# A conv-then-gated-MLP kernel: a reworked opening (tap broadcast, first cast, band copies, order of the first loads, first transposes)

## The chip, the cores and the metric

The kernel runs on one core of a Trainium2 chip. The metric is the device time of one execution in microseconds (us). Below, PE is the matrix engine, PEld its weight loads, DVE the vector engine, ACT the scalar engine, POOL is GpSimd, and SP the engine that only issues transfers here. "L415" is line 415 of the kernel before.

## What is computed

```
w   = softmax(weight, over the 7 taps)                  # weight [8 heads, 7]
y[b, s, c] = sum_k w[c // 24, k] * x[b, s - 6 + k, c]   # causal, zeros ahead of s = 0
h   = y.reshape(32768, 192) @ w_in                      # w_in [192, 2048]
out = (h * cos(h)) @ w_out                              # w_out [2048, 192], float32 result
```

x is [8, 4096, 192] float32. The reference adds 1e-9 to the softmax sum. The kernel computes in bf16 with float32 accumulation.

## The kernel before

The 32768 rows are cut into 64 tiles of T = 512 rows, and two tiles make a unit of 1024 rows; a unit has eight blocks of 128 rows. For each tile PE does eight first products h0 to h7 (`mm1`, L488; each takes 6 matmuls of 512 columns and fills two PSUM banks with 256 of the 2048 hidden features), ACT takes the cosine of each as Sin(h + pi/2) (L510), DVE multiplies (L514), and PE adds the second product in 64 steps (`mm2_step`, L523; steps 0 to 15 need the first half of w_out, step 16 is the first that needs the second half). What PE does in which order is written out by hand in strings (PE_FIRST for the first tiles, PE_ORDER later): "h3" is a first product, "m11" eleven steps of the second, "d11" or "c11" a part of the convolution of unit 1, "r" the second half of that of unit 0, "w5" five filler matmuls, "K1" two casts of unit 1 on POOL, "W0" and "W1" the casts of the halves of w_out on POOL, "X0" a DMA transpose of the second half of unit 0. ACT_FIRST and ACT_ORDER do the same for ACT ("s3" is the cosine of h3, "er" and "ed11" copies of the convolution out of PSUM).

The convolution is a product with a banded 128 x 256 matrix for each head (`band`), whose entries are the softmaxed taps. Units 0 to 3 are done on PE; the later ones are split between PE and POOL and are not touched by the change.

The change concerns what comes ahead of the first h0, called the opening here. In order:

- L80-81: ACT's queue loads the 56 taps as 4 rows of 14 (`w_row`); SP's queue loads the first four blocks of unit 0 (L102, called x0a here).
- L128-136: DVE clears `zero`; `keep_warm(n)` is n filler matmuls of 512 columns on it.
- L139-151: POOL makes `quarter` [4, 128] (a memset and two selects), PE runs three fillers, then one float32 matmul spreads the four rows of taps over the four quarters of 32 partitions (`w_all`), then nine fillers.
- L156-164: POOL makes `mask` on 32 partitions, DVE and ACT copy it to the other three quarters (ACT twice).
- L111-112, L165: POOL issues the two loads of w_in, which cast to bf16 on the way. L167-171: POOL clears a block and makes `ident`.
- L175-185: DVE and ACT do the softmax (max, subtract, Exp, sum, reciprocal, multiply into `wn`); ACT loads the Sin table behind its Exp.
- L398: ACT casts x0a to bf16. L400-404: DVE multiplies mask by taps (`prod`) and adds up (`diag`).
- L406-410: SP waits for `diag`, then issues the rest of unit 0 (called x0b here), unit 1 in two halves and its edges.
- L412-416: 16 copies of 32 x 76 put `diag` into `band`, four for each pair of heads (the pairs are taken one after another): the letters of "DPDPDPDPDPDPDPAA" give the engine (D for DVE, P for POOL, A for ACT).
- L417-421: POOL casts x0b and makes `pick`.
- `conv_first` (L426): PE convolves the first four blocks, in two halves of 16 matmuls; the first half needs all four pairs of heads of `band`. ACT copies half 0 out and DVE half 1 (L438), each value twice, into the two sets of columns t of `ct_tiles[0]`. SP waits for DVE's copy and then issues the four loads of w_out (L442-443, L124).
- `turn_first` (L445): PE transposes each block with three matmuls against `ident` (L453; the doubled values make all 128 output rows), ACT and DVE copy the result into cT (L457). Then the tiles begin: "K1 h0a h0b W0 h1 ...", where h0a and h0b are the two halves of h0.

All transfers issued by SP go through one queue in the order of issue.

Of the kernel before, what the change touches and what calls it, by code (L numbers as in the profile page):

```python
# [8 lines left out]
FP32 = mybir.dt.float32  # L9
# [7 lines left out]
def kernel(  # L17
# [61 lines left out]
    HQ = H // 4  # L79
    w_row = consts.tile([4, HQ * K], FP32)  # L80
    nc.scalar.dma_start(out=w_row, in_=weight.rearrange("(q h) k -> q (h k)", q=4))

# [44 lines left out]

    one = consts.tile([128, 1], FP32)  # L128
    nc.vector.memset(one, 1.0)
# [4 lines left out]
    def keep_warm(n, bank=idle):  # L134
        for _ in range(n):
            nc.tensor.matmul(out=bank, lhsT=zero[:, 0:128], rhs=zero, start=True, stop=True)  # L136


    quarter = consts.tile([4, 128], FP32)  # L139
    nc.gpsimd.memset(quarter, 1.0)  # L140
    nc.gpsimd.affine_select(out=quarter, in_=quarter, compare_op=ALU.is_ge, fill=0.0, base=0, pattern=[[1, 128]],
                            channel_multiplier=-32)
    nc.gpsimd.affine_select(out=quarter, in_=quarter, compare_op=ALU.is_ge, fill=0.0, base=31, pattern=[[-1, 128]],
                            channel_multiplier=32)
    scrap = consts.tile([128, 1], FP32)
    nc.scalar.activation(out=scrap, in_=one, func=AF.Exp)
    keep_warm(3)
    w_all = o_pools[1].tile([128, T], FP32, name="o_ps1")
    w_bc = w_all[:, 0 : HQ * K].rearrange("p (h k) -> p h k", k=K)
    nc.tensor.matmul(out=w_all[:, 0 : HQ * K], lhsT=quarter, rhs=w_row, start=True, stop=True)  # L150
    keep_warm(9)

# [26 lines left out]
    nc.scalar.activation(out=wexp, in_=wexp, func=AF.Exp)  # L179
    nc.scalar.activation(out=scrap, in_=one, func=AF.Sin)  # L180
    wsum = consts.tile([128, HQ, 1], FP32)
# [170 lines left out]
    def taps(u, j, half, mul):  # L352
        if u not in pa:
            pa[u] = pa_pool.tile([128, PA, WN, OR], FP32, name="pa")
        part = slice(HALF * half, HALF * (half + 1))
        mul(pa[u][:, j, part], tap_window(u, j)[:, part], tap[:, j : j + 1])  # L356
# [3 lines left out]
    def conv_raw(u):  # L360

        a, p = pa.pop(u), raw_prod
# [34 lines left out]

    cast_unit(0, 0, NB, nc.scalar.copy)  # L398

# [3 lines left out]
    diag = consts.tile([128, HQ, E], FP32)  # L403
    summed = nc.vector.tensor_reduce(out=diag, in_=prod, axis=mybir.AxisListType.X, op=ALU.add)  # L404

    tc.add_manual_dep(nc.sync.nop().ins, summed.ins.name, sync_dep, reason="order of the transfers")  # L406
    load_unit(0, NB, UB)
    load_unit(1, 0, NB)
    load_unit(1, NB, UB)
    load_edges(1)  # L410

    three = {"D": nc.vector.tensor_copy, "A": nc.scalar.copy, "P": nc.gpsimd.tensor_copy}  # L412
    for i, k in enumerate("DPDPDPDPDPDPDPAA"):
        q, rows = divmod(i, 4)
        three[k](out=band[32 * rows : 32 * rows + 32, HQ * q : HQ * (q + 1), 32 * rows : 32 * rows + E],  # L415
                     in_=diag[32 * q : 32 * q + 32])
    cast_unit(0, NB, UB)  # L417
# [8 lines left out]
    def conv_first():  # L426

        banks = o_banks()
        for half in range(2):
            for h in range(H):  # L430
                for prev in range(2):
                    nc.tensor.matmul(  # L432
                        out=banks[half][:, 0 : 2 * D].rearrange("p (n k h r) -> p h n k r", n=2, k=NC, h=H)[:, h],
                        lhsT=band[:, h, 128 * prev : 128 * prev + 128],
                        rhs=bf[0][:, 2 * half + 1 - prev : 2 * half + 3 - prev, h * G : (h + 1) * G].rearrange(
                            "p n (k r) -> p n k r", k=NC),
                        start=(h == 0 and prev == 0), stop=(h == H - 1 and prev == 1), skip_group_check=True)
            m = copies[half](out=ct_tiles[0][:, 2 * half : 2 * half + 2].rearrange("p n k t w -> p (n k) t w"),  # L438
                             in_=banks[half][:, 0 : 2 * D].rearrange("p (m t w) -> p m t w", t=1, w=64).to_broadcast(
                                 [128, 2 * NC, 2, 64]))  # L440
        tc.add_manual_dep(nc.sync.nop().ins, m.ins.name, sync_dep, reason="order of the transfers")
        load_wo(0)  # L442
        load_wo(1)

    def turn_first(half):  # L445
        for n in range(2):
            last = half and n
            ps = [o_pools[0].tile([128, T], FP32, name="o_ps0")] if last else ring_banks()
            if n == 0:
                keep_warm(2 - half, ps[1])  # L450
            ps = ps[0]
            for k in range(NC):
                nc.tensor.matmul(out=ps[:, k * 128 : (k + 1) * 128],  # L453
                                 lhsT=ct_tiles[0][:, 2 * half + n, k, :, :].rearrange("p t w -> p (t w)"), rhs=ident,
                                 start=True, stop=True, skip_group_check=True)
            m = NC * (2 * half + n)
# [131 lines left out]

    PE_ORDER = ['m12 h0 m4 h1 K+3 R+1 m5 h2 m7 q h3 U+0 m6 h4 m17 h5 X+1 m9 p h6 h7 O m4', 'm11 h0 m4 h1 m6 h2 m7 q x+1 h3 m5 h4 m7 c1 m8 c2 m3 h5 T+3 L+4 m9 p O h6 h7 m4']
    ACT_ORDER = ['s0 s1 a211 s2 s3 s4 a014 a114 Q s5 P s6 s7 a007', 's0 s1 s2 a102 s3 a203 s4 Q ec2 ec1 s5 P s6 s7']  # L590

    PE_FIRST = ["K1 h0a h0b W0 h1 h2 h3 r h4 w5 d11 w4 h5 d21 W1 c11 X0 m1 h6 m11 h7 L2 c21 D1",
# [5 lines left out]
    ACT_FIRST = ["s0a s0b s1 s2 er s3 s4 ed11 ed21 s5 ec11 s6 ec21 s7",  # L598
                "s0 s1 s2 s3 s4 s5 ec12 ec22 Q P s6 ed12 s7 ed22 ec13 ec23",
                "s0 s1 s2 s3 Q s4 P s5 s6 s7",  # L600
                "s0 s1 s2 s3 s4 ed13 ed23 Q s5 P s6 s7"] + ACT_ORDER

    PE_LAST = "m10 h0 m3 h1 m13 h2 m2 q h3 m10 h4 m3 h5 m7 h6 m12 p h7 O m7"
    ACT_LAST = "s0 s1 s2 s3 s4 s5 s6 P A s7"
# [7 lines left out]
    for t in range(NT + 1):  # L612
        u, second = divmod(t, TPU)
        cu = u + TPU
        if t >= 2 * TPU:
            if second:
                conv["c"] = conv_unit(cu, ring_banks) if cu < NU else iter(())
        pe = PE_LAST if t == NT - 1 else "m%d p" % (2 * STEPS * NT - step) if t == NT else PE_ORDER[second] if t >= len(PE_FIRST) else PE_FIRST[t]
        act = ACT_LAST if t == NT - 1 else ACT_ORDER[second] if t >= len(ACT_FIRST) else ACT_FIRST[t]
# [6 lines left out]
        def flush():  # L626
            while act:
                k = act[0]
                if k[0] == "e":
                    need = k[1:] if k[1:] in conv else k[1] + "2" + k[3:]  # L630
                else:
                    need = "p" if k in "PQA" else "h" + k[3:] if k[0] in "ab" else "h" + (k[1:2] if k[2:] in "lr" else k[1:])
                if need not in done:
# [5 lines left out]
                elif k[0] in "ab":  # L639
                    if u + 2 in rT:  # L640
                        taps(u + 2, int(k[1]), int(k[2]), nc.scalar.mul if k[0] == "a" else nc.vector.tensor_scalar_mul)
                elif k[0] == "e":
# [20 lines left out]
        for k in pe.split():  # L663
# [5 lines left out]
            elif k[0] == "m":  # L669
                for q in range(step, step + int(k[1:])):  # L670
                    mm2_step(q)
                step += int(k[1:])
            elif k[0] == "w":
                keep_warm(int(k[1:]), o_pools[0].tile([128, T], FP32, name="o_ps0"))
            elif k == "p":
                assert step % (2 * STEPS) == 0
                made = step // (2 * STEPS) - 1
            elif k == "q":
                assert step % (2 * STEPS) == STEPS
            elif k[0] == "W":  # L680
# [11 lines left out]
            flush()  # L692
            if k == "p" and made == NT - 1:
                finish(NT - 1)
        assert t == NT or not act
# [30 lines left out]
```

## Time and profile before

| | us |
|---|---|
| median of 3 runs | 705.16 (705.04 to 705.51) |
| the profiled execution, its own time | 705.18 |
| its span, first to last instruction | 703.5 |
| PE busy | 697.0 (99%) |
| ACT busy | 644.4 (92%) |
| DVE busy | 642.4 (91%) |
| POOL busy | 503.7 (72%) |
| first matmul of h0 | 10.60 after the start of the span |
| step 16 of the second product | 22.64 after the start of the span |

The span is divided by the profile into lines of instructions with a start, a duration, an engine, a line of the kernel and, in brackets, how long the engine was idle ahead of it and what ended that. The chain of waits is followed back from the last instruction: at each step to what released it, or to the instruction before it on its engine. The granted clock of PE was 0.999 of full speed over the span.

### The profile page before, as it was taken

To read this page: it belongs to the slowest core of one execution; us is meant where nothing else is said; L and a number is where in the kernel's file an instruction comes from. 1 tells how busy PE (TensorE), PEld (TensorE's weight loads), DVE (VectorE), ACT (ScalarE), POOL (GpSimd) and SP (SyncE) were. 2 spreads that over 40 slices of the span, in tenths; PEclk is the share of its full clock that TensorE was granted. 3 is DMA by queue.
4 is the path that set the end of the run, shared out by engine and by line. 5 is a ranking of instruction groups with operands and counts; after the bars stand their busy time and mean duration, and the time that the engine had idled before them with its cause. 6 is when DMAs were issued, how large, how long until landed. Compare 5 with 4: busy or idle time off the path is not lost.

```text
span 703.5 us, 26826 instructions
## 1 busy us (share of the span) xinstructions
PE 697.0 (99%) x11830; PEld 512.8 (73%) x11830; DVE 642.4 (91%) x598; ACT 644.4 (92%) x831; POOL 503.7 (72%) x214
## 2 busy tenths in 40 slices
PE   8999999999999999999999999999999999999997
PEld 4677777777777777777777777777777777777776
DVE  6889999999999999999999999999999999999996
ACT  7889999999999999999999999999999999999875
POOL 6524478977778877778877688877789778799400
PEclk9999999999999999999999999999999999999999
DMA  8964456667667768676656577577665576874331
GB/s 214 234 167 97 120 135 143 138 147 164 138 153 146 131 145 176 134 152 131 147 152 153 150 159 129 140 161 150 143 147 132 145 174 137 153 127 95 92 91 47
DMA packets 228292, 100.09 MB, mean 142 GB/s; under 512 B 156240, under 2 KB 227792, under 8 KB 228176
## 3 DMA queue, kind: packets, MB, share of 16 engines
q1 hardware_dynamic: 227464, 97.40, 62.7%
q8 instruction: 92, 1.51, 0.9%
q0 software_dynamic: 416, 0.79, 0.7%
q14 instruction: 24, 0.20, 0.1%
q10 hardware_dynamic: 296, 0.20, 0.1%
HBM read 31.36 MB, written 25.17 MB: 80 GB/s over the span
## 4 chain that ended last, share of the span: by engine, by line
PE 96%; DMA 1%; DVE 1%; POOL 0%; SPq 0%; ACT 0%; issue 0%; POOLq 0%
PE o_ps L552 48%; PE h L503 46%; PE h L277 2%; DMA wo_f<-in_moe_w_out_dram 1%; PE h L552 0%; SPq L124 0%; PE h L229 0%; DVE band L415 0%; POOL wo L120 0%; POOL mask L159 0%; DVE ct L438 0%; PE o_ps L432 0%; ACT mask L164 0%; DVE diag L404 0%; DVE prod L401 0%
## 5 line engine op out<-in xcount | busy, mean ns | idle before, releaser
L514 DVE TENSOR_TENSOR g<-h,cs 128x1024 bf16<-128x1024 f32 (+1 forms) x513 | 604.9, 1216 | 27.9 <-ACT cs L510 24.5
L510 ACT ACTIVATE cs<-h 128x1024 bf16<-128x1024 f32 (+1 forms) x513 | 511.0, 1021 | 44.0 <-PE h L503 30.6
L552 PEld LDWEIGHTS <-g 64*128 64x128 bf16 x8192 | 354.2, 94 | 102.2 <-issue 1.0
L552 PE MATMUL o_ps<-wo,g 64*128 64x192 bf16 x8128 | 420.6, 243 | 0.1
L503 PE MATMUL h<-cT,w 64*128 64x512 bf16 (+1 forms) x3078 | 407.0, 376 | 0.8 <-DVE g L514 0.4
L503 PEld LDWEIGHTS <-w 64*128 64x128 bf16 x3078 | 147.6, 94 | 75.0 <-issue 1.8
L211 POOL CAST xk<-x_f 128x768 bf16<-128x768 f32 (+1 forms) x56 | 76.4, 1367 | 113.9 <-DMA x_f<-in_x_dram 109.3
L363 POOL TENSOR_TENSOR raw_prod<-rT,tap 128x2784 f32<-128x2784 bf16 x28 | 135.3, 4832 | 0.2
L370 POOL TENSOR_TENSOR raw_prod<-raw_prod,pa 128x2088 f32<-128x2088 f32 x28 | 129.1, 4609 | 2.2
L356 ACT ACTIVATE pa<-rT,tap 128x348 f32<-128x348 bf16 x168 | 94.6, 580 | 0.0
L374 POOL TENSOR_TENSOR raw_prod<-raw_prod 128x1392 f32<-128x1392 f32 x28 | 87.9, 3138 | 2.2
L571 DVE COPY o_sb<-o_ps 128x384 f32<-128x384 f32 x62 | 34.6, 557 | 23.7 <-PE o_ps L552 23.5
L377 POOL TENSOR_TENSOR ro<-raw_prod 128x696 bf16<-128x696 f32 x28 | 46.5, 1660 | 2.2
L294 ACT CAST ct_buf<-h 112x480 bf16<-112x480 f32 x56 | 28.6, 562 | 4.1 <-PE h L277 0.6
L571 ACT COPY o_sb<-o_ps 128x384 f32<-128x384 f32 x64 | 30.8, 482 | 0.1
L277 PE MATMUL h<-xk,band 64*112 64x120 bf16 x448 | 21.2, 213 | 0.0
L277 PEld LDWEIGHTS <-band 64*112 64x112 bf16 x448 | 18.0, 127 | 0.0
L219 POOL CAST x_bf<-x_f 128x768 bf16<-128x768 f32 (+2 forms) x5 | 9.1, 1812 | 7.0 <-DMA x_f<-in_x_dram 6.9
L307 POOL COPY ct<-ct 128x1728 bf16<-128x1728 bf16 x3 | 4.9, 1630 | 8.9 <-ACT ct L239 8.9
L394 POOL COPY cT<-cT 128x144 bf16<-128x144 bf16 x3 | 0.9, 308 | 13.5 <-DMA cT<-ct 13.5
L136 PE MATMUL o_ps<-zero 128*128 128x512 bf16 x21 | 7.2, 492 | 1.3 <-DVE zero L131 1.3
L239 ACT CAST ct<-h 128x432 bf16<-128x432 f32 x12 | 5.9, 530 | 0.4 <-issue 0.4
(66 smaller groups left out, 52.7 us busy)
## 6 DMA issues: line engine op xcount, KB each, us to landing
out_dram<-o_sb SPq DMA_DIRECT2D x63, 384.0 KB, 3.7
x_f<-in_x_dram SPq DMA_DIRECT2D x28, 480.0 KB, 5.5
x_f<-in_x_dram SPq DMA_DIRECT2D x56, 192.0 KB, 2.7
cT<-ro SPq DMA_DIRECT2D x112, 87.0 KB, 2.3
x_f<-in_x_dram SPq DMA_DIRECT2D x4, 384.0 KB, 5.6
wo_f<-in_moe_w_out_dram SPq DMA_DIRECT2D x4, 384.0 KB, 7.9
x_f<-in_x_dram SPq DMA_DIRECT2D x2, 768.0 KB, 5.2
cT<-ct_buf SPq DMA_TRANSPOSE x56, 4.0
```

Source lines behind the costliest of these rows:

```text
L211: copy(out=xk[u][:, NC * n0 : NC * n1].rearrange("p (k n) m -> p k n m", k=NC), in_=x_tiles[u][:, n0:n1].rearrange("p n (m k) -> p k n m", ...
L277: return nc.tensor.matmul(out=ps[h // 4][0:OP, 0 : NPB * 4 * G].rearrange("p (m i r) -> p i m r", m=NC * NPB, i=4)[:, h % 4], lhsT=band[si ...
L356: mul(pa[u][:, j, part], tap_window(u, j)[:, part], tap[:, j : j + 1])
L363: nc.gpsimd.tensor_tensor(out=p, in0=tap_window(u, PA, K), in1=tap[:, PA:K].rearrange("p (j a b) -> p j a b", a=1, b=1).to_broadcast([128, ...
L370: add(out=p[:, 0:m], in0=p[:, 0:m], in1=a[:, done : done + m], op=ALU.add)
L374: add(out=p[:, 0:m], in0=p[:, 0:m], in1=p[:, n - m : n], op=ALU.add)
L377: add(out=ro[u], in0=p[:, 0], in1=p[:, 1], op=ALU.add)
L503: nc.tensor.matmul(out=h[:, i, n0 * 128 : n1 * 128], lhsT=w[rows, k, j, :], rhs=rhs, start=(k == 0), stop=(k == NC - 1))
L510: nc.scalar.activation(out=cs[:, :, part], in_=h[:, :, part], func=AF.Sin, bias=math.pi / 2.0, scale=1.0)
L514: nc.vector.tensor_tensor(out=g_tiles[t][:, 2 * j : 2 * j + 2, part], in0=h[:, :, part], in1=cs[:, :, part], op=ALU.mult)
L552: ms.append(nc.tensor.matmul(out=o_ps[tt, b, si], lhsT=g_tiles[tt][rows, f, s * 128 : (s + 1) * 128], rhs=wo[rows, f // 2, f % 2, :], star ...
L571: (copy or copies[b])(o_sb[t][:, 2 * b : 2 * b + 2, :].rearrange("p s d -> p (s d)"), o_ps.pop((t, b)))
```

## The change

- The taps are loaded into one partition as a row of 4 x 14. `quarter` and its three POOL instructions go; four float32 matmuls, one for each quarter of 32 output partitions, with a row of 32 ones as weights, take the place of the one. Eleven fillers follow, where there were nine.
- x0a is cast by POOL, where it was ACT.
- The 16 band copies go to DVE, ACT and POOL as "DAPDAPDAPDAPDADA" (6, 6 and 4), where it was 7, 2 and 7.
- SP's loads of x0b and unit 1 wait for the last band copy, where they waited for `diag`.
- `conv_first` copies each value out once (384 elements for each partition, where it was 768).
- `turn_first` transposes each block of 64 columns twice, into the output rows 0-63 and 64-127, so 24 matmuls with 64 columns of weights where there were 12 with 128. One filler stands ahead of each half, where there were two and one.
- The marks "p" and "q" in the order strings go; the end of a second product is found by counting steps. The order in which instructions are issued from the first tile on stays as it was.

```
-    w_row = consts.tile([4, HQ * K], FP32)
-    nc.scalar.dma_start(out=w_row, in_=weight.rearrange("(q h) k -> q (h k)", q=4))
+    w_row = consts.tile([1, 4, HQ * K], FP32)
+    nc.scalar.dma_start(out=w_row, in_=weight.rearrange("(o q h) k -> o q (h k)", o=1, q=4))
...
-    one = consts.tile([128, 1], FP32)
+    one = consts.tile([128, 32], FP32)
...
-    quarter = consts.tile([4, 128], FP32)
-    nc.gpsimd.memset(quarter, 1.0)
-    nc.gpsimd.affine_select(out=quarter, ...)
-    nc.gpsimd.affine_select(out=quarter, ...)
...
-    nc.tensor.matmul(out=w_all[:, 0 : HQ * K], lhsT=quarter, rhs=w_row, start=True, stop=True)
-    keep_warm(9)
+    for q in range(4):
+        nc.tensor.matmul(out=w_all[32 * q : 32 * q + 32, 0 : HQ * K], lhsT=one[0:1], rhs=w_row[:, q], start=True, stop=True)
+    keep_warm(11)
...
-    cast_unit(0, 0, NB, nc.scalar.copy)
+    cast_unit(0, 0, NB)
...
-    summed = nc.vector.tensor_reduce(out=diag, in_=prod, axis=mybir.AxisListType.X, op=ALU.add)
-    tc.add_manual_dep(nc.sync.nop().ins, summed.ins.name, sync_dep, reason="order of the transfers")
+    nc.vector.tensor_reduce(out=diag, in_=prod, axis=mybir.AxisListType.X, op=ALU.add)
+    three = {"D": nc.vector.tensor_copy, "A": nc.scalar.copy, "P": nc.gpsimd.tensor_copy}
+    for i, k in enumerate("DAPDAPDAPDAPDADA"):
+        q, rows = divmod(i, 4)
+        m = three[k](out=band[32 * rows : 32 * rows + 32, HQ * q : HQ * (q + 1), 32 * rows : 32 * rows + E],
+                     in_=diag[32 * q : 32 * q + 32])
+    tc.add_manual_dep(nc.sync.nop().ins, m.ins.name, sync_dep, reason="order of the transfers")
     load_unit(0, NB, UB)
     load_unit(1, 0, NB)
     load_unit(1, NB, UB)
     load_edges(1)
-    three = {...}
-    for i, k in enumerate("DPDPDPDPDPDPDPAA"):
...
-            m = copies[half](out=ct_tiles[0][:, 2 * half : 2 * half + 2].rearrange("p n k t w -> p (n k) t w"),
-                             in_=banks[half][:, 0 : 2 * D].rearrange("p (m t w) -> p m t w", t=1, w=64).to_broadcast(
-                                 [128, 2 * NC, 2, 64]))
+            m = copies[half](out=ct_tiles[0][:, 2 * half : 2 * half + 2, :, 0].rearrange("p n k w -> p (n k) w"),
+                             in_=banks[half][:, 0 : 2 * D].rearrange("p (m w) -> p m w", w=64))
...
-                keep_warm(2 - half, ps[1])
+                keep_warm(1, ps[1])
...
-                nc.tensor.matmul(out=ps[:, k * 128 : (k + 1) * 128],
-                                 lhsT=ct_tiles[0][:, 2 * half + n, k, :, :].rearrange("p t w -> p (t w)"), rhs=ident,
-                                 start=True, stop=True, skip_group_check=True)
+                for i in range(2):
+                    nc.tensor.matmul(out=ps[64 * i : 64 * i + 64, k * 128 : (k + 1) * 128],
+                                     lhsT=ct_tiles[0][:, 2 * half + n, k, 0, :], rhs=ident,
+                                     start=True, stop=True, skip_group_check=True)
```

More of the change, by code (lines that the diff above doesn't have):

```diff
@@ L136, in keep_warm @@
             nc.tensor.matmul(out=bank, lhsT=zero[:, 0:128], rhs=zero, start=True, stop=True)
-    quarter = consts.tile([4, 128], FP32)
-    nc.gpsimd.memset(quarter, 1.0)
[L141 to L144, printed above, removed]
     scrap = consts.tile([128, 1], FP32)
-    nc.scalar.activation(out=scrap, in_=one, func=AF.Exp)
+    nc.scalar.activation(out=scrap, in_=one[:, 0:1], func=AF.Exp)
     keep_warm(3)
@@ L179 @@
     nc.scalar.activation(out=wexp, in_=wexp, func=AF.Exp)
-    nc.scalar.activation(out=scrap, in_=one, func=AF.Sin)
+    nc.scalar.activation(out=scrap, in_=one[:, 0:1], func=AF.Sin)
     wsum = consts.tile([128, HQ, 1], FP32)
@@ L354, in taps @@
             pa[u] = pa_pool.tile([128, PA, WN, OR], FP32, name="pa")
+        have.add(("tap", u, j, half))
         part = slice(HALF * half, HALF * (half + 1))
@@ L360, in conv_raw @@
     def conv_raw(u):
+        assert {("tap", u, j, half) for j in range(PA) for half in range(2)} <= have
         a, p = pa.pop(u), raw_prod
@@ L410 @@
     load_edges(1)
-    three = {"D": nc.vector.tensor_copy, "A": nc.scalar.copy, "P": nc.gpsimd.tensor_copy}
-    for i, k in enumerate("DPDPDPDPDPDPDPAA"):
-        q, rows = divmod(i, 4)
-        three[k](out=band[32 * rows : 32 * rows + 32, HQ * q : HQ * (q + 1), 32 * rows : 32 * rows + E],
-                     in_=diag[32 * q : 32 * q + 32])
     cast_unit(0, NB, UB)
@@ L584 @@
     o_ps, o_sb, turns, evacs = {}, {}, {}, set()
-    PE_ORDER = ['m12 h0 m4 h1 K+3 R+1 m5 h2 m7 q h3 U+0 m6 h4 m17 h5 X+1 m9 p h6 h7 O m4', 'm11 h0 m4 h1 m6 h2 m7 q x+1 h3 m5 h4 m7 c1 m8 c2 m3 h5 T+3 L+4 m9 p O h6 h7 m4']
+    PE_ORDER = ['m12 h0 m4 h1 K+3 R+1 m5 h2 m7 h3 U+0 m6 h4 m17 h5 X+1 m9 h6 h7 O m4', 'm11 h0 m4 h1 m6 h2 m7 x+1 h3 m5 h4 m7 c1 m8 c2 m3 h5 T+3 L+4 m9 O h6 h7 m4']
     ACT_ORDER = ['s0 s1 a211 s2 s3 s4 a014 a114 Q s5 P s6 s7 a007', 's0 s1 s2 a102 s3 a203 s4 Q ec2 ec1 s5 P s6 s7']
     PE_FIRST = ["K1 h0a h0b W0 h1 h2 h3 r h4 w5 d11 w4 h5 d21 W1 c11 X0 m1 h6 m11 h7 L2 c21 D1",
[5 rows of a table removed]
[5 rows of a table added]
     ACT_FIRST = ["s0a s0b s1 s2 er s3 s4 ed11 ed21 s5 ec11 s6 ec21 s7",
@@ L600 @@
                 "s0 s1 s2 s3 Q s4 P s5 s6 s7",
-                "s0 s1 s2 s3 s4 ed13 ed23 Q s5 P s6 s7"] + ACT_ORDER
-    PE_LAST = "m10 h0 m3 h1 m13 h2 m2 q h3 m10 h4 m3 h5 m7 h6 m12 p h7 O m7"
[3 rows of a table added]
+    PE_LAST = "m10 h0 m3 h1 m13 h2 m2 h3 m10 h4 m3 h5 m7 h6 m12 h7 O m7"
     ACT_LAST = "s0 s1 s2 s3 s4 s5 s6 P A s7"
@@ L617 @@
                 conv["c"] = conv_unit(cu, ring_banks) if cu < NU else iter(())
-        pe = PE_LAST if t == NT - 1 else "m%d p" % (2 * STEPS * NT - step) if t == NT else PE_ORDER[second] if t >= len(PE_FIRST) else PE_FIRST[t]
+        pe = PE_LAST if t == NT - 1 else "m%d" % (2 * STEPS * NT - step) if t == NT else PE_ORDER[second] if t >= len(PE_FIRST) else PE_FIRST[t]
         act = ACT_LAST if t == NT - 1 else ACT_ORDER[second] if t >= len(ACT_FIRST) else ACT_FIRST[t]
@@ L631, in flush @@
                 else:
-                    need = "p" if k in "PQA" else "h" + k[3:] if k[0] in "ab" else "h" + (k[1:2] if k[2:] in "lr" else k[1:])
+                    need = "p" if k in "PQA" else "h" + k[3] if k[0] in "ab" else "h" + (k[1:2] if k[2:] in "lr" else k[1:])
                 if need not in done:
@@ L639, in flush @@
                 elif k[0] in "ab":
-                    if u + 2 in rT:
-                        taps(u + 2, int(k[1]), int(k[2]), nc.scalar.mul if k[0] == "a" else nc.vector.tensor_scalar_mul)
+                    v = int(k[4]) if k[4:] else u + 2
+                    if FIRST_RAW <= v < NU:
+                        taps(v, int(k[1]), int(k[2]), nc.scalar.mul if k[0] == "a" else nc.vector.tensor_scalar_mul)
                 elif k[0] == "e":
@@ L669 @@
             elif k[0] == "m":
-                for q in range(step, step + int(k[1:])):
-                    mm2_step(q)
-                step += int(k[1:])
+                for _ in range(int(k[1:])):
+                    mm2_step(step)
+                    step += 1
+                    if step % (2 * STEPS) == 0:
+                        made = step // (2 * STEPS) - 1
+                        done.add("p")
+                        flush()
+                        if made == NT - 1:
+                            finish(NT - 1)
             elif k[0] == "w":
                 keep_warm(int(k[1:]), o_pools[0].tile([128, T], FP32, name="o_ps0"))
[L675 to L679, printed above, removed]
             elif k[0] == "W":
@@ L692 @@
             flush()
-            if k == "p" and made == NT - 1:
-                finish(NT - 1)
         assert t == NT or not act
```

13 rows, old and new, of tables (ACT_FIRST, PE_FIRST) are left out of this document.

## The prediction

> **What bounds the kernel now.** I read the page's chain first, then the chain of waits of the first 45 us, then the timelines of the engines and the transfer slices up to 24 us. The page puts the end on PE:
>
> ```profile
> PE 96%; DMA 1%; DVE 1%; POOL 0%; SPq 0%; ACT 0%; issue 0%; POOLq 0%
> ```
>
> So a change of the opening is worth what it moves the point from which PE runs without a wait. The chain of waits (start, us, what) shows that point:
>
> ```profile
> 4.77 0.49 DVE prod L401
> ...
> 5.28 0.72 DVE diag L404
> ...
> 7.63 0.26 DVE band L415
> ...
> 8.19 0.69 PE o_ps L432 x20
> ...
> 8.90 0.97 DVE ct L438
> ...
> 12.16 8.84 DMA wo_f<-in_moe_w_out_dram
> ...
> 21.12 1.48 POOL wo L120
> ...
> 22.64 0.34 PE o_ps L552 x4
> ```
>
> From step 16 at 22.64 PE never lacks work again. It was released by the last w_out transfer, landed at 21.00, and its cast. But PE was ready only 0.26 us sooner: its 12 matmuls there start at 22.05, the first eight (steps 12 to 15) need 8 x 0.041 (26 take 1.07 in the chain), so to 22.38. A second bound therefore lies close by, the ACT timeline:
>
> ```profile
> 11.14 3.26 ACT L510 ACTIVATE cs<-h 128x512 bf16<-128x512 f32 x4 [0.37 <-PE h L503]
> 14.47 1.50 ACT L472 CAST ct<-o_ps 128x768 bf16<-128x768 f32 x2
> 15.86 1.96 ACT L510 ACTIVATE cs<-h 128x1024 bf16<-128x1024 f32 x2
> 17.68 0.97 ACT L239 CAST ct<-h 128x432 bf16<-128x432 f32 x2
> ```
>
> ACT is busy from the first cosine to 22.3 but for gaps of about 0.4. The time thus falls by the smaller of two shifts: that of h0a (10.60, after cT at 10.46), and that of the stream of transfers. For the second, the view of transfers between 6 and 9 us:
>
> ```profile
> q0 software_dynamic: 225, 0.43, 94.4%
> ```
>
> Only w_in's packets (q0) move, at 94% of the engines, though SP issued x0b at 6.01. x0b flows from about 9.4, when w_in is nearly done (in, by its row, at most 6.6 after the issue at 3.8: 10.4).
>
> **The change, part by part.**
>
> *Taps.* Three POOL instructions go (L140 at 0.82; mask started at 1.67): POOL is 0.85 earlier, mask ready at 2.17, w_in issued at 2.13, landed at 9.55. ACT's mask copies then wait for its table load and scrap instead (end 2.89): 2.92 to 3.75, where they ended at 3.88. Against this stand four float32 matmuls for one. This one's row:
>
> ```profile
> L150 PEld LDWEIGHTS o_ps<-w_row,quarter x2: 284/308/332, 2.7 to 2.9; 4*128 4x128 f32 x2
> L150 PE MATMUL o_ps<-w_row,quarter x2: 368/378/387, 2.7 to 2.9; 4*128 4x14 f32 x2
> ```
>
> One is two passes, the second 0.22 behind the first; so eight passes now. No row shows 32 columns of weights. Bounds of the spacing: 0.04 (the 24 of L432 in 0.98) and 0.22. I take 0.08, a quarter of the 0.308 load for a quarter of the columns. The last pass starts at 2.71 + 7 x 0.08 = 3.27 and ends at 3.64 (before 3.30). From there maximum and subtraction take 0.45 (3.30 to 3.75), so Exp starts at 4.09, before 3.91: +0.18 (bounds -0.10 and +1.16). Everything down to `diag` follows Exp: its end T0 = 6.00 + 0.18 = 6.18. The wider `one` adds at most 0.03 to the first filler, nothing taken. Two more fillers: PE ends them at 7.2 to 7.9 (6.72, +0.34, +0.2 to 0.85); the last band copies, below, come at 7.83, so they hide; at 7.9 they would cost 0.1, plus up to 0.5 for band matmuls queued behind.
>
> *x0a's cast.* POOL is free at 5.40 - 0.85 = 4.55. A 128x768 cast there took 1.23, so 4.6 to 5.83, before T0. ACT did not wait for x0a at 5.55, and the slices show its data in by 3.6. ACT is free at Exp + 1.73 = 5.82. What the cast does to DVE beside it is a rival.
>
> *Band copies.* Seven on POOL took 2.00 (0.286 each), seven on DVE 1.86 (0.27 with the gaps), two on ACT 0.51. Now DVE 6 x 0.27 = 1.62, ACT 6 x 0.26 = 1.56, POOL 4 x 0.286 = 1.15: all done at T0 + 1.65 = 7.83, where the last pair came at 8.16 (PE's 8.19). Alone, a DVE copy took 0.188: at best T0 + 1.3; were the three to slow each other as much again as two do (0.188 to 0.27), +0.4. Hence -0.33.
>
> *The hold of x0b and unit 1.* SP issues at 7.83, not 6.01. An issue needs about 1.2 to flow (x0a: 0.82, slices full from 2.0), so 9.05. w_in, 0.85 earlier, leaves the engines free from about 9.0. The cover is w_in itself: each 0.1 by which the band comes later than 7.8 costs 0.1 of the stream. Queued behind on SP are w_out's loads: x0b to edges took 6.01 to 8.52, so w_out is issued from 10.35, not 9.89; its data's turn comes only about 4 us after x0b's, so this hides. x0b then flows from 9.05 where I put 9.4 to 9.9 mixed with w_in: -0.65 for it (POOL's cast 11.73 to 11.1) and all behind it.
>
> *Copied out once.* 128x768 took 0.80 on ACT and 0.96 on DVE; 128x384 out of PSUM took 0.52 and 0.56 (L457). Half 0: 7.83 + 0.31 (8.19 to 8.50) + 0.52 = 8.66, was 9.30. Half 1: 7.83 + 0.71 + 0.56 = 9.10, was 9.86.
>
> *Column halves.* 24 matmuls of 128 columns for 12; before, six took 0.34 of PE. If a pair runs side by side, as the row halves of L503 do (six of 512 columns in 0.65, half of six times 0.213), nothing is added; one behind the other adds 0.17 for a block. I take nothing, the nearest row being a pair of halves. Then the first copy starts 8.70 + 0.38 = 9.08 (before 9.35 to 9.73), DVE's 9.25 to 9.81 (was 9.90 to 10.46): h0a 0.65 earlier, 9.95; h0b's copy ends 10.37, was 11.02. The Trainium skill speaks against this: TensorEngine Tiling (Array Packing), sections "Key Properties" and "Restrictions", says that a change of tiling mode drains TensorE and that column tiling disables fast weight load. By it I would lean to the serial end, 0.2 to 0.35 more for h0a; no row of before has column halves.
>
> *Rest.* The removed order marks issue nothing. Unit 1's casts on POOL move with x0b, the d11 matmuls (16.62) with them; ACT reads them at 17.68.
>
> **Sum.** h0a -0.65, the stream -0.65, step 16 at 21.99: 705.18 (the profiled execution; span 703.5 plus 1.68 around it) - 0.65 = 704.5; the median of the runs is 705.16, the same within 0.02. A measurement of this kernel tells about 0.2% from no change, 1.41 us here.
>
> **Rivals.**
>
> 1. *POOL's cast holds up DVE (slower).* `wn` and `prod` read two SBUF operands each while POOL reads x0a. If they wait, `wn` starts at 5.83, not 4.74: T0 = 7.27, band 8.92, h0a +0.44, x0b's flow 10.15 (+0.5 to +0.75). Time +0.45 to +0.75, 705.8; it decides once the cast starts ahead of `wn`, 4.6 against 4.74. For it: the DVE copies at L415 stretch from 0.188 to 0.29 beside POOL's. Against: `prod` took 0.48 beside POOL's select of `ident`, which took 0.50, neither one held for the other's length. The Trainium skill, SBUF — State Buffer, section "Who interferes with whom", states this rule: a vector instruction with two SBUF inputs and a GpSimd one that reads SBUF exclude each other, and the first one holds the port to its end. Chance 0.22; with more waits of that kind or late casts of unit 1 behind, +1.4 and over, 0.09 of it.
> 2. *The float32 passes cost their full 0.22, halves run serially.* Exp 5.07, T0 7.16, h0a +0.5: 705.8. Chance 0.10, past +1.41 in 0.05.
> 3. *The last w_out transfer is not earlier.* Its data trickles at 27 GB/s between 19.0 and 20.5, beside the transpose X0; if that place is fixed, step 16 stays: 705.2. Chance 0.08.
> 4. *Everything near the good bounds.* Passes at 0.04, copies at 0.19: T0 5.90, h0a at w_in's landing 9.6 (-1.0), PE's 0.26 at step 16 gone: -1.26, 703.9. For it: nothing in the trace forbids it. Chance 0.22, past -1.41 in 0.15, if gaps of ACT (0.4 each) close too.
>
> My forecast has 0.38, 0.05 of it past -1.41. So faster by over 0.2% 0.20, slower 0.14, within 0.66. The range takes in rivals 1 and 4 with part of their tails: 703.6 to 706.3; the likeliest case alone 704.1 to 704.9.
>
> **What would show it.** Eight passes ending by 3.7 and Exp near 4.1; POOL's cast 4.6 to 5.9 with `wn` starting within 0.7 of Exp (if it starts at the cast's end, rival 1); last band copy near 7.8; x0b flowing by 9.1 with no hole behind w_in; h0a near 9.95; the cast of w_out's second half at 20.5; step 16 near 22.0. I am wrong if h0a is early and step 16 is not, or if the PE chain after 22 us has new waits.

## The result and the profile after

| | us |
|---|---|
| before, median of 9 runs | 705.16 (705.01 to 705.51) |
| after, median of 9 runs | 706.94 (706.12 to 707.65) |
| ratio after to before, 95% interval | 1.0026 (1.0018 to 1.0035) |
| the profiled execution of after, its own time | 707.65 |
| its span | 705.9 (before 703.5) |

The change costs 1.78 us; the forecast was a gain of 0.65, and the range ended at 706.3. The profiled execution is the slowest of the nine: its span is 2.4 longer than that of before. Of this, 1.8 is there at DVE's last multiply, which starts at 697.64 (695.84 before); the other 0.6 lies behind it, where the last issue of the output takes 0.94 (0.36 before), and was not followed. PE still sets the end. The chain by engine, from the page of after:

```profile
PE 96%; DMA 1%; ACT 1%; DVE 1%; POOL 0%; SPq 0%; issue 0%; ACTq 0%; POOLq 0%
```

ACT stands third in it, where it was sixth. Where it comes in is seen in the chain of waits of after (start, us, what):

```profile
4.33 1.17 DVE wn L180
...
6.04 0.72 DVE diag L401
...
8.13 0.26 ACT band L406
8.41 0.38 SPq L102
...
9.94 7.18 DMA x_f<-in_x_dram
...
17.23 1.49 POOL x_bf L214
...
18.76 0.53 PE h L224 x4
...
21.00 1.03 ACT cs L506
...
23.33 0.83 PE h L499 x6
```

In the chain of before the transfer on the path was w_out's last. Now it is unit 1's x, by its last transfer, the edges: the last band copy ends at 8.39, only then SP issues x0b and unit 1, the edges go out at 9.94 and are in at 17.1, POOL casts the second half of unit 1 with them, and PE's part d11 of the convolution starts at 18.76. In before d11 and h7 started about 2 us earlier (the timeline of before):

```profile
16.62 0.53 PE L229 MATMUL h<-x_bf,band 128*128 128x216 bf16 x4
...
21.41 0.82 PE L503 MATMUL h<-cT,w 64*128 64x512 bf16 x6 [0.15 <-DVE g L514]
```

ACT, which has to copy d11 out, shows the hole in after:

```profile
11.33 3.26 ACT L506 ACTIVATE cs<-h 128x512 bf16<-128x512 f32 x4 [0.40 <-PE h L499]
14.66 1.50 ACT L468 CAST ct<-o_ps 128x768 bf16<-128x768 f32 x2
16.04 1.96 ACT L506 ACTIVATE cs<-h 128x1024 bf16<-128x1024 f32 x2
19.37 0.94 ACT L234 CAST ct<-h 128x432 bf16<-128x432 f32 x2 [1.36 <-PE h L332]
```

The first cosine is 0.19 later than before (11.14), not 0.65 earlier, and then ACT is idle for 1.36 where it had run on. h7 starts at 23.33.

The transfers between 6 and 9 us look as before, full of w_in:

```profile
q0 software_dynamic: 231, 0.42, 90.9%
```

Behind them they do not. The busy share of the DMA engines from 8 to 11 us, 40 slices of 0.075 us, one digit each; first the view of before:

```profile
DMA  4696975998989999999797979899999999999999
```

and the same view of after:

```profile
DMA  8999989291714031121634943425275889999999
```

Before, x0b's packets had long been queued when w_in ran out, and no slice shows a hole. After, from 8.6 to 10.3 us most slices are under half: w_in's last packets trickle on some of the engines (20% of the engines' time from 9.0 to 9.5), and x0b has hardly begun (5%).

The taps went as meant, and better. The view of their line in after (minimum, median and maximum in ns):

```profile
L145 PEld LDWEIGHTS o_ps<-w_row,one x8: 123/138/151, 2.6 to 2.7; 1*32 1x32 f32 x8
L145 PE MATMUL o_ps<-w_row,one x8: 208/218/228, 2.6 to 2.7; 1*32 1x14 f32 x8
```

Eight passes, all started within 0.1, and the last ends at 2.94, earlier than the two of before (3.30). But then the timelines of POOL and of DVE in after:

```profile
4.25 1.21 POOL L214 CAST x_bf<-x_f 128x768 bf16<-128x768 f32 x1
```

```profile
4.33 1.16 DVE L180 TENSOR_TENSOR wn<-wexp,winv 128x14 bf16<-128x14 f32 x1
5.53 0.47 DVE L398 TENSOR_TENSOR prod<-mask,wn 128x532 bf16<-128x532 bf16 x1
6.04 0.71 DVE L401 TENSOR_REDUCE diag<-prod 128x76 f32<-128x532 bf16 x1
```

`wn`, 14 elements from each partition, takes 1.16 and ends 0.03 after POOL's cast of x0a; without the cast beside it, it takes 0.17 (below).

### The profile page after: what moved, and what is told of

It is laid out like the page before. It is cut to its first block, busy times and chain, and to the rows that moved or that the text cites. A ratio compares the mean times of both kernels' runs of the same rounds, so it can differ in the third digit from the quotient of the medians.

```text
span 705.9 us, 26857 instructions
## 1 busy us (share of the span) xinstructions
PE 696.4 (99%) x11847; PEld 513.8 (73%) x11849; DVE 643.0 (91%) x597; ACT 643.8 (91%) x834; POOL 503.1 (71%) x209
## 4 chain that ended last, share of the span: by engine, by line
PE 96%; DMA 1%; ACT 1%; DVE 1%; POOL 0%; SPq 0%; issue 0%; ACTq 0%; POOLq 0%
PE o_ps L548 47%; PE h L499 46%; PE h L272 2%; DMA x_f<-in_x_dram 1%; PE h L548 0%; PE h L224 0%; ACT band L406 0%; POOL x_bf L214 0%; SPq L102 0%; ACT L140 0%; DVE g L510 0%; DVE wn L180 0%; ACT cs L506 0%; PE o_ps L136 0%; ACT mask L159 0%
```

## The experiments

Four theories are numbered in the expectations. Theory 1: POOL's cast of x0a holds up DVE's two-operand `wn`. Theory 2: the hold of x0b and unit 1 behind the last band copy opens a hole in the stream. Theory 3: w_in, issued earlier, lands no earlier and unevenly; 3a gives as its cause that its start overlaps x0a's tail on the same DMA engines. Theory 4: PE has more instructions ahead of the first tile, so its next fetch of instructions, in the traces one packet of 16 KB that takes about 1.1, falls into the loads of w_out. Each run is compared with runs of before on the same chip (705.07 to 705.12 in the four groups; 705.16 beside after). A trace shows one execution, a median mostly eleven: the traces of the first run below and of the run with the three memsets alone are of executions 0.5 faster than their medians. "Landing marks" are the moments at which the 16 DMA engines report their share of a transfer in the trace.

### Undoing the lock and the hold

After, with x0a's cast made to wait for `prod`:

```
+    def cast_held(**k):
+        c = nc.gpsimd.tensor_copy(**k)
+        tc.add_manual_dep(c.ins, prod_i.ins.name, sync_dep, reason="cast behind prod")
+
+    cast_unit(0, 0, NB, cast_held)
```

> The changed kernel with one edit: POOL's cast of x0a waits for DVE's prod, so it no longer runs beside the two-operand wn and prod. Theory 1 (the cast holds DVE up for 1.0 us and everything follows): wn back to 0.17 us, diag ends near 5.8 instead of 6.75, the last band copy near 7.4 instead of 8.39, x0b issued at 7.4 and flowing by 8.9 with no hole behind w_in; d11 no longer waits for the cast of unit 1; time 704.6 to 705.2, at least 1.5 below the changed kernel. Theory 2 (the hold of x0b and unit 1 costs by itself, whatever the band's time): the loads still go out 1.4 later than before, d11 near 17.8, time 705.8 to 706.3. Theory 3 (w_in, issued 0.9 earlier beside x0a's tail, leaves some DMA engines more than 1 us late, and the edges of unit 1 land behind them): the edges still land near 16.5 to 17, d11 near 18.5, time 706 to 707.

Measured: 706.07, ratio 1.0015 (1.0006 to 1.0024). `wn` is short again, and `diag` ends 1.0 earlier at 5.75:

```profile
4.33 0.17 DVE L180 TENSOR_TENSOR wn<-wexp,winv 128x14 bf16<-128x14 f32 x1
```

So Theory 1's lock is real, and the difference of the medians to after is 0.87. But the run is still 1.0 slower than before, and h0a now waits for w_in, whose marks are spread from 8.66 to 11.02.

After, with SP waiting for `diag` again:

```
-    tc.add_manual_dep(nc.sync.nop().ins, m.ins.name, sync_dep, reason="order of the transfers")
+    tc.add_manual_dep(nc.sync.nop().ins, summed.ins.name, sync_dep, reason="order of the transfers")
```

> The changed kernel with one edit: SP waits for diag again, not for the last band copy. wn still waits 1.0 us for POOL's cast. x0b is issued at 6.8 instead of 8.4. Theory 2 (the hold): x0b flows from about 9, as w_in ends, the edges land near 15, d11 near 16.7 to 17.0; h0a stays at 10.55, so the time is 705.2 to 705.5, back at the kernel before. Theory 1 (DVE's wait passed on by everything): only the transfers gain, h0a and ACT stay 0.2 late: 705.3 to 706. Theory 3 (uneven engines): edges still after 16.3, time 706 to 707.

Measured: 705.50, 1.0007 (0.9998 to 1.0016). With the lock left in, this alone takes back 1.44 of the 1.78.

Both together:

> The changed kernel with both edits: POOL's cast behind prod, SP waits for diag. Theories 1 and 2: diag near 5.8, h0a bound by w_in's landing or by the copies near 9.7 to 9.9, x0b flowing by 8.5 to 9, d11 near 16; time 704.3 to 704.7, below the kernel before. If theory 1 alone holds, it equals the cast behind prod alone within 0.3; if theory 2 alone holds, it equals the run without the hold within 0.3. Theory 3: the edges land after 16 and d11 after 18 in both, time over 705.5.

Measured: 705.83, 1.0011 (1.0003 to 1.0020). Without the hold, removing the lock brings nothing more that can be told (705.50 and 705.83, intervals overlapping). So the lock cost its time through the hold: it made the band late, and the hold passed that on to the stream. w_in's last mark is at 10.92, and the chain goes through w_out's first half, cast from 18.77 (17.35 before).

The hold alone on the kernel before, behind POOL's last band copy (8.15):

```
-    tc.add_manual_dep(nc.sync.nop().ins, summed.ins.name, sync_dep, reason="order of the transfers")
+    tc.add_manual_dep(nc.sync.nop().ins, last.ins.name, sync_dep, reason="order of the transfers")
```

(with the loads moved behind the band copies)

> The kernel before with one edit: SP's loads of x0b and unit 1 wait for POOL's last band copy (end 8.15) instead of diag (6.00). Theory 2: x0b flows from about 9.7 instead of 9.4; w_in still ends at 9.9, so the hole is small: 0.2 to 0.5 later for d11, time 705.2 to 705.7. Theories 1 and 3 alone: the same as before within 0.2, since w_in covers the wait. If the hold costs by its order alone (w_out's issues pushed back behind it), w_out's second half lands 1 us late or more and the time is 706 or over.

Measured: 706.32, 1.0017 (1.0008 to 1.0026): +1.25 with no lock and with w_in in at 10.42 as before. The hold costs by itself, and more than Theory 2 expected (705.2 to 705.7). x0b, the first behind it on SP's queue, lands at 13.18 (11.61 before), so the hole is there. The chain of waits goes through w_out's first half, which is behind x0b and unit 1 on that queue:

```profile
11.16 8.47 DMA wo_f<-in_moe_w_out_dram
19.75 1.48 POOL wo L120
```

In before that cast started 2.4 earlier:

```profile
17.35 1.47 POOL L120 CAST wo<-wo_f 128x1536 bf16<-128x1536 f32 x1 [0.78 <-DMA wo_f<-in_moe_w_out_dram]
```

Of these 2.4, 1.3 come from one DMA engine: its mark comes at 19.63, the fifteenth at 18.37, with PE's fetch at 17.3 (see Theory 4 below). What the hole alone costs, what the later issue of w_out and what the fetch that the late stream now meets, the runs do not part.

### w_in issued earlier

The taps in a row alone on the kernel before, which brings POOL's issue of w_in forward by 0.9:

```
-    w_row = consts.tile([4, HQ * K], FP32)
+    w_row = consts.tile([1, 4, HQ * K], FP32)
...
+    for q in range(4):
+        nc.tensor.matmul(out=w_all[32 * q : 32 * q + 32, 0 : HQ * K], lhsT=one[0:1], rhs=w_row[:, q], start=True, stop=True)
```

> The kernel before with the taps in one row (four float32 matmuls, no quarter on POOL), nothing else; nine fillers as before. w_in is issued 0.85 earlier, diag ends near 5.75 instead of 6.00. If an earlier issue brings w_in earlier (what the prediction took): landed by 9.6, h0a bound by the copies at 10.3, time 704.7 to 704.9. Theory 3 (some DMA engines keep w_in until the same time or later, however early it is issued): last landing mark 10.3 to 11.0, h0a at 10.5 to 11.1, the edges and w_out later by 0.2 to 0.6, time 705.1 to 705.7.

Measured: 706.11, 1.0014 (1.0005 to 1.0023), +1.0, more than Theory 3 expected. The part of the change that shortens the path to `diag` makes the kernel slower by itself. The marks of w_in's second part lie between 8.78 and 11.51; before, between 9.69 and 10.42. h0a needs all of them, and the chain of this run says so:

```profile
2.86 8.65 DMA w<-in_moe_w_in_dram
11.55 0.51 PE h L498 x5
```

After, without hold and lock, and with three spare memsets on POOL ahead of w_in's issue, so that it goes out 0.9 later, as before:

```
+    spare = consts.tile([128, 192], BF16)
+    for _ in range(3):
+        nc.gpsimd.memset(spare, 0.0)
     for t in range(2):
         load_w(t)
```

> The changed kernel without the hold, POOL's cast behind prod, and three spare POOL memsets (0.28 each) ahead of the loads of w_in, which so go out at 2.9 as before. Theory 3 (the early issue beside x0a's tail makes w_in uneven): w_in's landing marks close up again (9.7 to 10.4), the edges land by 15.0, time 704.8 to 705.2, 0.6 or more below the same kernel with the early issue (705.83). If the unevenness has another cause, or the fetch of instructions is what costs: still 705.5 to 706.

Measured: 705.10, 1.0000 (0.9991 to 1.0009): with w_in 0.9 later the kernel is 0.73 faster than without the memsets. The marks are even again, 9.54 to 10.48. Yet nothing is won against before, though the transposed unit 0 (cT) is ready at 9.78, 0.7 earlier. The chain of this run:

```profile
3.79 6.70 DMA w<-in_moe_w_in_dram
10.53 0.51 PE h L506 x5
```

All of h0a's matmuls but the first start when w_in is in, at 10.53; in before h0a started at 10.60.

The three memsets alone on after, hold kept and no wait added:

> The changed kernel with one edit: three spare POOL memsets ahead of the loads of w_in (out at 3.0 instead of 2.06), so POOL's cast of x0a starts near 5.15, behind the start of prod, without any wait being added; the hold of x0b stays. Theory 3 (the early w_in is what makes the stream uneven) together with theory 1 (the cast holds up wn only when it starts first): wn back at 0.17, diag near 5.75, band 7.6, x0b issued at 7.6 and flowing by 9.6, w_in even and landed by 10.5; time 705.1 to 705.6, 1.3 or more below the changed kernel. If the hold costs 1.2 by itself, as in the kernel before with the hold alone: 706.0 to 706.5.

Measured: 705.63, 1.0007 (0.9999 to 1.0016), so 1.31 better than after from three spare memsets. They also move x0a's cast behind `wn` (0.18), and SP issues x0b at 7.42, not 8.41; so this run undoes Theory 1 and 3 together and cannot part them. With the run before it, it gives the price of a shorter hold: released at 7.42, the hold costs 0.53 (705.63 against 705.10), and 0.24, not clear of the spread, where w_in is early (706.07 against 705.83). Released at 8.15 and 8.41 it cost 1.25 and 1.44.

To part the causes of Theory 3, the run with even marks (the memsets, no hold, no lock) with x0a issued 1.0 later, at 1.76, so that its tail lies on w_in's start again:

```
-    load_unit(0, 0, NB)
...
-    nc.vector.memset(band, 0.0)
+    cleared = nc.vector.memset(band[:, 0 : H // 2], 0.0)
+    nc.vector.memset(band[:, H // 2 : H], 0.0)
+    tc.add_manual_dep(nc.sync.nop().ins, cleared.ins.name, ..., reason="first load later")
+    load_unit(0, 0, NB)
```

> The best kernel so far (changed, no hold, cast behind prod, w_in at 3.0; 705.10) with one edit: SP's first load, x0a, waits for the first half of DVE's clearing of band, so it goes out near 1.85 instead of 0.76 and its tail again falls on w_in's start. Theory 3a (w_in beside x0a's tail on the same DMA engines is what makes w_in uneven): marks of w_in spread to 10.8 or later, h0a at 10.9 or later, time 705.5 to 706.2. Theory 3b (the early issue itself is bad, for example through what DVE does while POOL writes the descriptors): w_in even and in by 10.6, time 705.0 to 705.3.

Measured: 708.47, 1.0051 (1.0038 to 1.0063). x0a lands 1.0 later, and w_in, issued as late as in the even run, has marks from 9.46 to 12.95. From the chain of waits:

```profile
3.69 9.27 DMA w<-in_moe_w_in_dram
13.00 4.31 PE h L509 x29
```

The overlap with the tail of x0a makes w_in uneven: 3a stands. All thirteen traces with w_in in its two whole parts agree. In the six in which its first packet starts before x0a's last has ended (after: 3.65 against 3.84; here: 4.53 against 4.86), the marks of its second part are 1.9 to 3.5 apart; in the seven in which it starts later (before: 4.51 against 3.83), 0.7 to 1.0. The size was not foreseen: 3a expected 706.2 at most, and of the 3.4 to the even run the later start of h0a's bulk (13.00 against 10.53) accounts for 2.5. What happens on a DMA engine that has both was not seen.

### What PE's side of the opening is worth

The copy-out once and the column halves, with one filler ahead of each half, alone on the kernel before:

```
...
-                nc.tensor.matmul(out=ps[:, k * 128 : (k + 1) * 128],
-                                 lhsT=ct_tiles[0][:, 2 * half + n, k, :, :].rearrange("p t w -> p (t w)"), rhs=ident,
...
+                for i in range(2):
+                    nc.tensor.matmul(out=ps[64 * i : 64 * i + 64, k * 128 : (k + 1) * 128],
+                                     lhsT=ct_tiles[0][:, 2 * half + n, k, 0, :], rhs=ident,
...
```

> The kernel before with the copies out done once and the transposes in column halves, nothing else. The first copies end 0.3 to 0.4 earlier, cT near 10.0 instead of 10.46; w_in still lands at 10.42. If h0a was held by the copies: 704.6 to 704.9. If h0a was held by w_in as much as by the copies: h0a stays near 10.55 and only h0b gains (11.07 to 10.7); ACT starts its cosines no earlier, time 704.9 to 705.2, the same as before.

Measured: 705.34, 1.0005 (0.9996 to 1.0014): no difference that can be told. h0a waits for w_in (0.37 of idle weight loads, to 10.73), and the chain goes through the first half of w_out:

```profile
9.90 8.81 DMA wo_f<-in_moe_w_out_dram
```

Here Theory 4 shows: PE's fetch comes at 15.5 (17.0 before), fifteen engines have delivered that half of w_out by 17.26, the sixteenth at 18.71 (17.00 and 17.23 before).

Theory 4 by itself, on the kernel before: nine fillers of 512 columns cut into 27 of 171, which gives PE 36 more instructions.

```
-    keep_warm(9)
+    for _ in range(27):
+        nc.tensor.matmul(out=idle[:, 0:171], lhsT=zero[:, 0:128], rhs=zero[:, 0:171], start=True, stop=True)
```

> The kernel before with the nine fillers of 512 columns cut into 27 of 171 columns: the same columns and the same work for PE, but 36 more PE instructions, as many as the change adds. PE's first fetch of 16 KB of instructions, at 17.0 before, should come near 15, as in the runs of the changed kernel. Theory 4 (this fetch takes one of the 16 DMA engines for about 1 us, and in the middle of w_out's first half it holds up its cast W0): w_out's first half lands 0.8 or more later, W0 at 18.2 or later, time 705.4 to 705.9. If the fetch does not matter: 705.0 to 705.2.

Measured: 705.35, 1.0004 (0.9995 to 1.0013). The fetch comes at 14.8, the sixteenth mark at 18.16 beside 17.13 for the fifteenth: with the instructions alone both come, the earlier fetch and the late engine. In before, with the fetch at 17.0, it is the next load of w_out whose sixteenth mark is late (19.90, the fifteenth at 18.23), and there nothing waits for it. That it is the engine of the fetch was not seen, only that the two go together. What it costs, +0.23, is within what can't be told from nothing.

### w_in in parts

If w_in's landing alone holds h0a, its first feature half, which is all that h0a needs, should be loaded first. The even run, with the second half issued behind the band copies:

```
-    def load_w(t):
+    def load_w(t, j0=0, j1=HP):
...
     for t in range(2):
         load_w(t)
...
+    for t in range(2):
+        load_w(t, HP, NP)
```

> The best kernel so far with w_in loaded in two halves of features: the first half (h0 to h3) at 3.0, the second half issued by POOL behind its band copies, near 7.6. If h0a is held by w_in alone (10.53, cT there at 9.8): the first half lands by 8.5, h0a starts at 9.85, ACT's cosines 0.65 earlier; time 704.3 to 704.8, below both kernels. If the stream of transfers is the bound: h0a early, but w_out's halves no earlier or later than 17.7, time 705.0 to 705.6.

Measured: 708.29, 1.0050 (1.0038 to 1.0063). The first half is in by 8.04, h0a starts at 9.90 and the first cosine at 10.44 (11.14 before). But the second half, 0.39 MB, issued as two loads at 7.55 and 8.20 beside SP's loads, is in only at 17.07. The chain:

```profile
8.20 8.87 DMA w<-in_moe_w_in_dram
17.11 0.82 PE h L509 x5
```

The same without the spare memsets:

> As the run with w_in in two halves, but without the spare memsets, so the first half goes out at 2.06. Theory 3: the half that runs beside x0a's tail is uneven again, but ends by 9 at the latest, ahead of cT, so h0a is not held; the unevenness only passes to x0b. Time 704.4 to 705.2, no better than with the later issue.

Measured: 708.03, 1.0038 (1.0024 to 1.0051); the second half takes from 7.50 to 16.05.

Two more runs keep the parts in one unbroken order. Both are after without hold and lock, with `ident` made ahead of w_in (which delays its issue as the memsets did) and band copies 7, 7 and 2. The first issues w_in in four parts, the first feature half of both t ahead of the second:

```
-    for t in range(2):
-        load_w(t)
...
+    for j in (0, HP):
+        for t in range(2):
+            load_w(t, j, j + HP)
```

> The kernel after, without the hold (SP waits for diag, as before), x0a's cast behind prod, ident and the cleared block made on POOL ahead of w_in, band copies 7 on DVE, 7 on ACT, 2 on POOL, and w_in issued in four parts: first feature half of both t, then the second half of both, one behind the other on POOL's queue, all ahead of SP's later loads. If h0a is held by the landing of the whole of w_in alone (10.42 to 10.5 in every run with an even landing), the first half lands by about 8.2 and h0a starts at 9.9 to 10.1, 0.5 earlier than before, the second half is in by 11 and nothing else is later: 704.6 to 704.8 (-0.3 to -0.5). If the stream of x0b, unit 1 and w_out sets the time instead, h0a is earlier but step 16 is not: 705.0 to 705.3. If the two further issues of POOL (0.7 each) delay x0a's cast past the band copies, h0a comes at 10.4 or later: 705.1 to 705.8.

Measured: 706.16, 1.0016 (1.0007 to 1.0025).

The second issues it whole:

> The same with w_in in its two whole parts, as before: the control for the ordered halves. w_in lands evenly by 10.3 to 10.5 and holds h0a there: 705.1, as before (704.9 to 705.3), if the landing of w_in holds h0a; if the halves change nothing, it is equal to the run with ordered halves.

Measured: 705.17, 1.0000 (0.9992 to 1.0009). In parts, the first half is in only at 9.21 and the whole at 11.82; whole, at 10.37. Four issues keep POOL for 2.66 where two take 1.43, and the last part then meets x0b, which is in at 12.80 (11.59 whole) and lies on the chain of that run. So the parts cost more than they free. h0a starts at 10.41 in parts, bound by cT (10.26 there, since DVE's seven band copies stretch to 2.37), and at 10.34 whole, with cT at 10.20 and w_in at 10.37. In the whole version cT is late for another reason, at the start of its chain:

```profile
2.94 4.79 PE o_ps L136 x11
...
7.86 1.05 PE o_ps L432 x32
```

PE was busy with its eleven fillers until after the last band copy (7.66), and all 32 products of the convolution came behind them. In the even run the fillers ended at 6.84, and cT was ready at 9.78; in after they ended at 6.13. The spacing of the fillers falls from 0.43 to 0.21 at a moment that differs from trace to trace; why was not followed. The prediction's "so they hide" thus held in after, but not in every run.

What was to be told apart, whether w_in's landing alone holds the gain back, is thus not told by the parts. The whole version has h0a 0.26 earlier than before and POOL's cast of x0b at 11.71 (11.73 before), and its time is that of before. Its chain:

```profile
9.95 7.87 DMA wo_f<-in_moe_w_out_dram
17.94 1.48 POOL wo L120
```

The next thing late is w_out's first half, whose sixteenth mark comes at 17.82, the others by 17.04; the fetch is at 14.5 here. By the medians none of the versions beats the kernel before.

## Why the prediction was wrong, step by step

**The hold of x0b and unit 1: the step that failed.** The prediction said "An issue needs about 1.2 to flow" and "The cover is w_in itself", and took -0.65 for the stream. Issued at 8.41 in after, x0b shows in 54% of the engines' time between 10.0 and 10.5 and fills them from 10.5: 2.1 after its issue, not 1.2. x0a, from which I took the 1.2, was misread in the same way: issued at 0.82 in before, its share is 8.1% from 1.5 to 2, 78.0% from 2 to 2.5 and over 83% only then. And w_in covers nothing at its end, for it thins out engine by engine: in after 13 of its last 16 marks lie between 8.82 and 9.40, the other three between 10.22 and 10.75. So the cover ended at 8.6, not at 9.05, and by my estimate x0b had to be issued by about 6.5 (8.6 less 2.1; before issued it at 6.01). In place of -0.65 the step costs 1.25 alone (the hold on the kernel before), and undoing it in after gives back 1.44.

**"w_in issued at 2.13, landed at 9.55": why nothing is won without the hold either.** The issue was right (2.06). The landing was not: 10.75 in after, 10.42 before. I moved the landing with the issue as if the transfer were of fixed length. Its start now lies beside x0a, which lands by 4.19, and three engines finish 0.8 to 1.9 us behind the others. Taps alone: +1.0.

**x0a's cast on POOL.** The prediction put it "before T0" and made the lock a rival at 0.22. The lock decided, as that rival said: the cast started at 4.25 (4.6 forecast), `wn` at 4.33 (4.74). `wn` took 1.16 beside the cast, 0.17 without. The rule of the Trainium skill (SBUF — State Buffer, "Who interferes with whom") agrees with this trace. What I held against it, POOL's select of `ident` beside `prod`, was misread: it took 0.50 there, but 0.29 in after, where no two-operand instruction of DVE ran beside it:

```profile
3.97 0.29 POOL L165 TENSOR_SCALAR_AFFINE_SELECT ident<-ident 128x128 bf16<-128x128 bf16 x1
```

So the row of before already showed a delay of 0.21, though no run tests that it is the same lock. The rival's sum, +0.45 to +0.75, is near the 0.87 of removing the lock; but that price holds only with the hold in place.

**Taps.** I took +0.18 for the passes; they ended 0.36 earlier than the one before, and Exp started at 3.68, not 4.09. It was then bound by ACT's mask copies (to 3.66). So the sign was wrong: Exp came 0.23 earlier than before, not 0.18 later. The lock then took more than this.

**Band copies.** T0 + 1.65 predicted; from `diag` at 6.75 to 8.39 is 1.64. Right.

**Copied out once.** 0.52 and 0.56 predicted, 0.48 and 0.56 measured.

**Column halves.** I took nothing added; twelve matmuls of half the width take 0.53 for a pair of blocks that took six matmuls and 0.51 before. So the 0.2 to 0.35 that I had put at the serial end did not come. What the Trainium skill states (TensorEngine Tiling (Array Packing), "Key Properties" and "Restrictions": a drain at the change of mode, no fast weight load) had made me weigh it; these rows show no such cost beyond 0.02.

**The sum.** "The time thus falls by the smaller of two shifts" was the right frame, but h0a has a third bound that I had set aside by shifting it: w_in's landing at 10.4 to 10.5. In before, cT (10.46) and w_in (10.42) came together, so nothing on PE's side could bring more than 0.05. Rival 4 named that bound, but at 9.6. The hold, the lock and the early issue of w_in then turned no gain into a loss. How the 1.78 divides depends on the order of undoing: the hold 1.44 first or the lock 0.87 first, and w_in's issue the most of what is left (0.73 between the runs without hold and lock). What stays open: what becomes of the opening's remaining gain. In the last run's trace, an execution of 704.89, h0a is 0.26 earlier than before and DVE's last multiply 0.46 earlier (695.38), so there the gain lasts to the end; yet the median of that run is 705.17. How much the earlier fetch or the fillers take in the other executions is not shown; alone the fetch was too small to measure.

## What to carry to other kernels

Before shortening a path, list every input of the instruction at its end with its landing time: a transfer that lands 0.04 before the computed input caps the gain at that. Do not hold back a transfer until the one ahead of it ends; queue it well before the first engine runs dry (2.1 us from issue to full slices here). A load issued earlier is not landed earlier when its start falls on another load's tail: look at when the last of the engines reports, not at the mean.

## What the runs showed of the hardware that I had not expected

- Three memsets that do nothing, ahead of the issue of a load, made the kernel without hold and lock 0.73 faster (705.83 to 705.10): the load went out 0.9 later and landed 0.4 earlier (10.92 to 10.48).
- A load issued by POOL that casts on the way is slow beside other traffic: from the first issue to the last mark 0.39 MB took 9.5 us beside SP's queue (7.55 to 17.07), the whole 0.79 MB 7.5 with little beside it (2.98 to 10.48).
- After a fetch of PE's instructions, one packet of 16 KB, one DMA engine's share of a load comes 0.8 to 1.7 behind the other fifteen (18.71 against 17.26 with the copies and halves alone), and a cast that needs all sixteen waits for it. 36 more PE instructions moved the fetch from 17.0 to 14.8.
- Eight float32 passes with 32 columns of weights to four different quarters took 0.30 together, about 0.2 for each alone; they overlap almost wholly.
